# Weight rounding in place in four steps, and activation in ten lagged steps with two groups in flight

## The chip, the cores and the metric

The kernel runs on one core of a Trainium2 chip. Its time is the device time in microseconds of one execution; three runs of the kernel before gave 877.65, 879.63 and 879.96 us. The engines are TensorE (PE; its weight loads are PEld), VectorE (DVE), ScalarE (ACT), GpSimd (POOL) and SyncE (SP, which issues most DMAs).

## The reference

Two stages follow one another. The first is a gated recurrence for 4 batches, 8 heads, 768 steps and a head size of 48; its output, with heads side by side, is a matrix of 3072 rows and 384 columns. The second is a two-layer network with a softplus-erf activation:

```
f = 1 / (1 + exp(-f_logit))
state = f[t] * state + outer(k[t], v[t]);   y[t] = q[t] @ state
h = x @ w_in                      # 3072x384 @ 384x2048
g = h * erf(softplus(h))
out = g @ w_out                   # 3072x2048 @ 2048x384
```

The inputs q, k, v and f_logit are float32; the two weight matrices are float64.

## The kernel before, in words

**Blocks, chunks, groups.** The 3072 rows are cut into 8 blocks of 384, a block into 3 chunks of 128. For a chunk the recurrence is written as matrix products in four stages: `stage_d` (cumulated log gates through a triangular matmul, their exponentials `dp` and `dm`, and the scaled `qd` and `kd`), `stage_t` (transposes of `qd` and `kd` into `qT` and `kT`), `stage_s` (scores `sc`, masked into `A`, and the state's update `dS`, `Sn`, `Mbd`) and `stage_y` (the chunk's output, copied by ScalarE to `xT`). `prepare` and `prepare_log` take exp and log of a whole block's gates. In the network a block has 16 tiles of 128 hidden columns, in 4 groups of 4. `hidden` makes a group: 12 matmuls, and after each six a VectorE copy of two tiles from PSUM (`hps`, two buffers) into one of 7 buffers `Hg`. `activate` runs on a group of 128 x 1536 values: exp and log on ScalarE, four squares on ScalarE (L150), each followed by a product on VectorE (L155), tanh, and a last product. `project` multiplies a block's groups with `w_out`: 16 matmuls for each of three row tiles, a ScalarE copy `osb` and a DMA out.

**Slots.** The order of every instruction on every engine is written out by hand (a manual schedule); no planner moves anything. A loop over blocks `it` draws from `slots(it)`, a generator that issues one matmul of the network at a time: 48 slots in block 0 (its four groups), 96 in later blocks (three groups of block `it`, the projection of block `it - 1`, the fourth group), 48 in a last pass that only projects. Between slots the loop issues stages of the next block's chunks at even distances (some 7 slots in a full block), activation steps (`act_step`), loads, and in block 0 the rounding of the weights. Each engine runs what it was given in that order and waits where data is missing. When `project` needs a group that isn't activated yet, it issues activation steps until it is.

**Activation before.** `act_step` runs on every odd slot and advances the oldest group to its next `yield`; the next group starts when it has ended. A group takes 16 slots, so the four groups of a block take 64 of 96. A square and the product of the square before it are issued in one step. The squares have two buffers, tag `x`.

**Rounding before.** Each float64 weight arrives as two 32-bit words in a raw piece of 128 x 768 values (16 pieces, 8 of `w_in`, 8 of `w_out`), loaded into `Hg` buffers that activation doesn't use yet; `raw_buf` says which. `round_piece` makes float32 of it: `Abs` on ScalarE and a clamp on GpSimd into a scratch tile that takes the same two `x` buffers as the squares, then on VectorE four instructions with masks, shifts and a product (L239 to L249), and an add into the weight tile, on VectorE for `w_in`, on GpSimd for `w_out` (L254). `weights_step` ends the piece before and begins the next; when a piece has ended, its buffer is loaded with a later one.

Of the kernel before, what the change touches and what calls it, by code (L numbers as in the profile page):

```python
# [65 lines left out]
P = 128  # L66
# [3 lines left out]
def kernel(  # L70
# [18 lines left out]
    DP = 64  # L89
# [73 lines left out]
    work = main.enter_context(tc.tile_pool(name="work", bufs=2))  # L163
    work1 = main.enter_context(tc.tile_pool(name="work1", bufs=1))
# [40 lines left out]
    raw_buf = [0, 1, 2, 3, 4, 5, 6, 4, 5, 6, 4, 5, 6, 4, 5, 6]  # L205
# [17 lines left out]
    def round_piece(i):  # L223

        dst, raw = raws.pop(i)
        if wpe == 1:
            return
        words = raw.rearrange("p (n two) -> p n two", two=2)  # L230
        low, high = words[:, :, 0], words[:, :, 1]
        t = work.tile([P, 2, PIECE], U32, name="w_t", tag="x")
        x, z = t[:, 0, :], t[:, 1, :]
        nc.scalar.activation(out=x.bitcast(FP32), in_=high.bitcast(FP32), func=AF.Abs)  # L234
        nc.gpsimd.tensor_scalar(  # L235
            out=x.bitcast(FP32), in0=x.bitcast(FP32), scalar1=TINY, scalar2=None, op0=ALU.max
        )
        yield
        nc.vector.tensor_scalar(  # L239
            out=x, in0=x, scalar1=0x07FFFFFF, scalar2=3,  # L240
# [3 lines left out]
            out=x, in0=high, scalar=0xC0000000, in1=x, op0=ALU.bitwise_and, op1=ALU.bitwise_or  # L244
# [31 lines left out]
    def stage_d(g):  # L276
# [5 lines left out]
        dp = dps[g % 2]  # L282
# [11 lines left out]
            out=qds[g % 2][:, :, 0:D].rearrange("t (a r) d -> t a r d", r=2),  # L294
# [103 lines left out]

    def act_step():
# [8 lines left out]
    def hidden(blk, gi):  # L408

        gr = {"h": Hgs[n_made[0] % NG], "done": False}  # L410
        assert all(j < ended[0] for j, x in enumerate(raw_buf) if x == n_made[0] % NG)
        n_made[0] += 1
        groups[blk, gi] = gr
        for u in range(FG // 2):
            hps = ps_moe.tile([P, 2, 512], FP32, name="hps", tag="moe")
            for j in range(2):
                ft = gi * FG + 2 * u + j
                for kt in range(n_k):
# [6 lines left out]
                    if j == 1 and kt == n_k - 1:  # L425
                        nc.vector.tensor_copy(  # L426
# [68 lines left out]
    with tc.manual_schedule():  # L495
# [26 lines left out]
        for t in dps:  # L522
# [325 lines left out]
```

## Time and profile before

| | |
|---|---|
| median of 3 runs | 879.63 us (877.65 to 879.96) |
| the profiled execution | 878.28 us |
| its span, first to last instruction | 876.6 us |
| mean granted TensorE clock | 0.903 |
| busy: TensorE, ScalarE, VectorE, GpSimd | 684.9, 533.3, 504.7, 146.5 us |

A profile shows one execution. Busy times are unions of instructions, so engines overlap and their shares don't add to one. "Idle before" is the time for which an engine stood just ahead of an instruction, and the arrow names what released it. The clock is a share of TensorE's full speed. L12 is line 12 of the kernel.

### The profile page before, as it was taken

The page shows a single profiled execution, that of the slowest core. Times are in us where ns is not written, and L with a number is a line of the kernel's source. Part 1 is how long each engine was busy: PE and PEld are TensorE (multiplying, and loading weights), DVE is VectorE, ACT ScalarE, POOL GpSimd, SP SyncE. Part 2 cuts the span into 40 slices and gives each one's busy share as a digit, 9 for nine tenths or more (in the row PEclk, how much of TensorE's full clock was granted, in tenths as well). Part 3 has the DMA queues.
Part 4 walks back from the last instruction along what each step waited for, and adds up shares of the span by engine and source line. Part 5 has one row for each costly group of instructions (what it writes and reads, how often), then busy time and mean ns, then how long its engine had stood idle before and what let it go on. Part 6 is the DMA issues. An engine that isn't in the chain of part 4 may idle for free.

```text
span 876.6 us, 9159 instructions
## 1 busy us (share of the span) xinstructions
PE 684.9 (78%) x3729; PEld 410.2 (47%) x3729; DVE 504.7 (58%) x429; ACT 533.3 (61%) x457; POOL 146.5 (17%) x95
## 2 busy tenths in 40 slices
PE   3756636376888987978698886978698879989696
PEld 2524423244555554644455553644455545545353
DVE  3968775577562884277552884266552875185440
ACT  5264634277975779178745779178744776389450
POOL 2433445501210130000310130000310010000000
PEclk9868868779899899999899998999899999989999
DMA  9913145200113001400033001400030000000000
GB/s 222 261 49 93 45 105 147 35 1 0 37 37 63 1 1 37 99 0 1 1 73 63 1 1 37 99 0 1 1 73 10 1 0 19 10 1 0 18 10 30
DMA packets 112176, 36.88 MB, mean 42 GB/s; under 512 B 103936, under 2 KB 107008, under 8 KB 112128
## 3 DMA queue, kind: packets, MB, share of 16 engines
q1 hardware_dynamic: 108672, 36.18, 17.2%
q8 instruction: 31, 0.51, 0.2%
q10 hardware_dynamic: 3456, 0.05, 0.2%
q14 instruction: 17, 0.14, 0.1%
HBM read 31.46 MB, written 4.72 MB: 41 GB/s over the span
## 4 chain that ended last, share of the span: by engine, by line
ACT 29%; DVE 26%; PE 26%; issue 12%; POOL 4%; DMA 1%; ACTq 0%; SPq 0%; DVEq 0%; POOLq 0%
DVE e L155 17%; PE ops L445 15%; PE hps L419 7%; ACT x L150 5%; ACT yl L381 4%; ACT e L379 4%; ACT L381 3%; ACT e L394 3%; POOL w_out_sb L254 2%; ACT dp L285 2%; ACT L285 1%; PE y L144 1%; DVE Hg L426 1%; POOL w_t L235 1%; DVE qd L293 1%
## 5 line engine op out<-in xcount | busy, mean ns | idle before, releaser
L419 PE MATMUL hps<-xT,w_in_sb 128*128 128x384 f32 x768 | 290.9, 531 | 71.5 <-DVE Hg L426 65.1
L155 DVE SCALAR_TENSOR_TENSOR e<-x,e 128x1536 f32<-128x1536 f32 x128 | 244.2, 1908 | 109.7 <-ACT x L150 103.6
L445 PE MATMUL ops<-w_out_sb,Hg 128*128 128x384 f32 x768 | 274.0, 512 | 0.6 <-ACT osb L453 0.6
L419 PEld LDWEIGHTS hps<-xT,w_in_sb 128*128 128x128 f32 x768 | 154.4, 207 | 189.4 <-DVE Hg L426 71.8
L150 ACT ACTIVATE x<-yl,serf_bias 128x1536 f32<-128x1536 f32 x128 | 199.4, 1573 | 62.6 <-DVE e L155 44.3
L445 PEld LDWEIGHTS ops<-w_out_sb,Hg 128*128 128x128 f32 x768 | 151.6, 201 | 106.1 <-issue 19.5
L426 DVE COPY Hg<-hps 128x768 f32<-128x768 f32 x64 | 60.8, 951 | 94.5 <-PE hps L419 94.3
L298 POOL TENSOR_TENSOR kd<-kn,dm 128x384 f32<-128x384 f32 x24 | 32.6, 1360 | 421.6 <-ACT dm L289 257.2
L379 ACT ACTIVATE e<-Hg 128x1536 f32<-128x1536 f32 x32 | 47.2, 1475 | 63.9 <-DVE Hg L426 62.7
L394 ACT ACTIVATE e<-e 128x1536 f32<-128x1536 f32 x32 | 47.4, 1483 | 54.8 <-DVE e L155 53.8
L396 DVE TENSOR_TENSOR Hg<-Hg,e 128x1536 f32<-128x1536 f32 x32 | 62.3, 1946 | 22.0 <-ACT e L394 21.9
L293 DVE TENSOR_TENSOR qd<-qn,dp 128x384 f32<-128x384 f32 x24 | 20.6, 859 | 87.9 <-ACT dp L285 87.4
L279 PE MATMUL ps_d<-lt,tri 128*128 128x384 f32 x48 | 25.4, 617 | 40.0 <-ACT lt L274 40.0
L311 PE MATMUL ps_t<-ident,kd 128*128 128x128 f32 x96 | 19.4, 339 | 42.0 <-DVE Sn L356 38.9
L144 PE MATMUL y<-A,vt 128*32 128x128 f32 x768 | 39.0, 295 | 16.4 <-DVE kT L316 15.1
L381 ACT ACTIVATE yl<-e 128x1536 f32<-128x1536 f32 x32 | 47.5, 1483 | 0.4
L359 POOL TENSOR_TENSOR Mbd<-Sn,Tall 48x192 f32<-48x192 f32 x32 | 30.3, 947 | 99.7 <-DVE Sn L356 98.5
L144 PEld LDWEIGHTS y<-A,vt 128*32 128x32 f32 x768 | 29.4, 115 | 29.7 <-DVE kT L316 17.1
L235 POOL TENSOR_SCALAR w_t<-w_t 128x768 f32<-128x768 f32 x16 | 37.3, 2332 | 26.8 <-ACT w_t L234 26.7
L381 ACT ACT_TABLE_LOAD x32 | 41.1, 1283 | 0.6
L370 ACT COPY xT<-y 128x384 f32<-128x384 f32 x24 | 11.3, 471 | 43.8 <-PE y L144 43.8
L234 ACT ACTIVATE w_t<-Hg 128x768 f32<-128x768 f32 x16 | 14.3, 903 | 35.9 <-POOL w_out_sb L254 28.6
(53 smaller groups left out, 496.2 us busy)
## 6 DMA issues: line engine op xcount, KB each, us to landing
Hg<-in_moe_w_in_dram SPq DMA_DIRECT2D x8, 768.0 KB, 6.7
Hg<-in_moe_w_out_dram SPq DMA_DIRECT2D x8, 768.0 KB, 4.4
lt<-in_f_logit_dram SPq DMA_DIRECT2D x24, 192.0 KB, 3.6
qn<-in_q_dram SPq DMA_DIRECT2D x24, 192.0 KB, 3.6
kn<-in_k_dram SPq DMA_DIRECT2D x24, 192.0 KB, 3.8
vt<-in_v_dram SPq DMA_DIRECT2D x24, 192.0 KB, 3.8
out_dram<-osb SPq DMA_DIRECT2D x24, 192.0 KB, 2.0
Tall<-dp ACTq DMA_DIRECT2D x24, 2.0 KB, 2.0
```

The source lines that it names most:

```text
L144: nc.tensor.matmul(y[M * i : M * (i + 1), kt, :], lhsT=terms[n][0], rhs=terms[n][1], start=(n == 0), stop=(n == len(terms) - 1), skip_grou ...
L150: nc.scalar.activation(out=dst[:], in_=y[:], func=AF.Square, bias=serf_bias[:, i : i + 1], scale=SERF_K)
L155: nc.vector.scalar_tensor_tensor(out=e[:], in0=x[:], scalar=SERF_AB[i][1], in1=e[:], op0=ALU.add, op1=ALU.mult)
L235: nc.gpsimd.tensor_scalar(out=x.bitcast(FP32), in0=x.bitcast(FP32), scalar1=TINY, scalar2=None, op0=ALU.max)
L298: nc.gpsimd.tensor_tensor(out=kds[g % 2][:, :, 0:D], in0=kns[g % NQ][:].rearrange("t (h d) -> t h d", d=D), in1=dm[:].rearrange("t (h d) - ...
L379: nc.scalar.activation(out=e[:], in_=h, func=AF.Exp)
L381: nc.scalar.activation(out=y[:], in_=e[:], func=AF.Ln, scale=SERF_C, bias=1.0)
L394: nc.scalar.activation(out=e[:], in_=e[:], func=AF.Tanh)
L396: nc.vector.tensor_tensor(out=h, in0=h, in1=e[:], op=ALU.mult)
L419: nc.tensor.matmul(hps[:, j, 0:TB], lhsT=w_in_sb[:, kt, ft * P : (ft + 1) * P], rhs=xTs[blk][:, kt, :], start=(kt == 0), stop=(kt == n_k - 1),
L426: nc.vector.tensor_copy(out=gr["h"][:, 2 * u : 2 * u + 2, :], in_=hps[:, :, 0:TB])
L445: nc.tensor.matmul(of[tt], lhsT=gr["h"][:, ft % FG, tt * P : (tt + 1) * P], rhs=w_out_sb[:, ft, :], start=(ft == 0), stop=(ft == n_ft - 1),)
```

## The change

- **Rounding** uses no scratch: `Abs` writes into the weight tile itself, the clamp and the masks work there, and the masked exponent goes back into the raw words (`high`, every second word). Its parts lie in separate steps: `Abs`; clamp; the four VectorE instructions; the add. The add is VectorE's for the first three pieces and GpSimd's for the other 13. `weights_step` advances every piece in flight by one step. Buffers for the pieces are given out in another order.
- **Activation** has ten steps: exp; log; four squares with the products two steps behind them, over six steps; tanh; the last product. A second group starts when the first has done six steps, and both are advanced in one `act_step`. Squares have three buffers of their own (`xpool`). Steps come on every third slot in blocks 0 and 1, on every fourth afterwards, and on every slot in the last pass.
- `qd` and `dp` have one buffer instead of two.
- Loads of the gates of block 1 are issued ahead of the fourth weight piece, q, k, v of chunks 3 and 4 within the first chunks' stages, and exp and log of block 1's gates before `stage_y(2)`; the stages of block 0 start at slot 3 instead of 12.

```diff
+    xpool = main.enter_context(tc.tile_pool(name="xpool", bufs=3))
...
-    qds = [fixed(f"qd{i}", [P, H, DP], pool=fix) for i in range(2)]
+    qd = fixed("qd", [P, H, DP], pool=fix)
-    dps = [fixed(f"dp{i}", [P, 2, DP, HP], pool=fix) for i in range(2)]
+    dp = fixed("dp", [P, 2, DP, HP], pool=fix)
...
-    raw_buf = [0, 1, 2, 3, 4, 5, 6, 4, 5, 6, 4, 5, 6, 4, 5, 6]
+    FIRST_PIECES = 3
+    raw_buf = [0, 1, 2, 3, 4, 5, 6, 3, 4, 5, 6, 4, 5, 6, 4, 5]
...
     def round_piece(i):
-        words = raw.rearrange("p (n two) -> p n two", two=2)
-        low, high = words[:, :, 0], words[:, :, 1]
-        t = work.tile([P, 2, PIECE], U32, name="w_t", tag="x")
-        x, z = t[:, 0, :], t[:, 1, :]
-        nc.scalar.activation(out=x.bitcast(FP32), in_=high.bitcast(FP32), func=AF.Abs)
-        nc.gpsimd.tensor_scalar(
-            out=x.bitcast(FP32), in0=x.bitcast(FP32), scalar1=TINY, scalar2=None, op0=ALU.max
-        )
+        m = dst.shape[1]
+        words = raw.rearrange("p (a n two) -> p a n two", a=m, two=2)
+        low, high = words[:, :, :, 0], words[:, :, :, 1]
+        bits = dst.bitcast(U32)
+        nc.scalar.activation(out=dst, in_=high.bitcast(FP32), func=AF.Abs)
+        yield
+        nc.gpsimd.tensor_scalar(out=dst, in0=dst, scalar1=TINY, scalar2=None, op0=ALU.max)
         yield
...
         nc.vector.tensor_scalar(
-            out=z, in0=x, scalar1=0xFF800000, scalar2=None, op0=ALU.bitwise_and
+            out=high, in0=bits, scalar1=0xFF800000, scalar2=None, op0=ALU.bitwise_and
         )
...
-        eng = nc.vector if i < n_pieces else nc.gpsimd
-        eng.tensor_tensor(
-            out=dst,
...
+        if i >= FIRST_PIECES:
+            yield
+        (nc.vector if i < FIRST_PIECES else nc.gpsimd).tensor_tensor(
+            out=dst, in0=low.bitcast(FP32), in1=dst, op=ALU.add
         )
...
     def activate(gr):
         nc.scalar.activation(out=e[:], in_=h, func=AF.Exp)
+        yield
         y = work1.tile([P, FG * TB], FP32, name="yl", tag="yl")
         nc.scalar.activation(out=y[:], in_=e[:], func=AF.Ln, scale=SERF_C, bias=1.0)
         yield
-        x = None
-        for i in range(len(SERF_AB)):
-            x_new = work.tile([P, FG * TB], FP32, name="x", tag="x")
-            squared(x_new, y, i)
-            if x is not None:
-                times(e, x, i - 1)
-            x = x_new
+        n = len(SERF_AB)
+        xs = {}
+        for i in range(n + 2):
+            if i < n:
+                xs[i] = xpool.tile([P, FG * TB], FP32, name="x", tag="x")
+                squared(xs[i], y, i)
+            if i >= 2:
+                times(e, xs.pop(i - 2), i - 2)
             yield
-        times(e, x, len(SERF_AB) - 1)
-        yield
-        yield
         nc.scalar.activation(out=e[:], in_=e[:], func=AF.Tanh)
         yield
         nc.vector.tensor_tensor(out=h, in0=h, in1=e[:], op=ALU.mult)
...
+    LEAD = len(SERF_AB) + 2
+    running = []
     def act_step():
-        while acts:
-            if next(acts[0], "end") != "end":
-                return
-            acts.popleft()
+        if acts and (not running or running[-1][1] >= LEAD):
+            running.append([acts.popleft(), 0])
+        for r in list(running):
+            r[1] += 1
+            if next(r[0], "end") == "end":
+                running.remove(r)
...
-        next_piece(5)
+        for g in range(CPB, 2 * CPB):
+            load_f(g)
+        next_piece(2)
...
-        def weights_step():
-            if rounding:
-                next(rounding.popleft(), None)
-                ended[0] += 1
-                next_piece()
-            if begun[0] < 2 * n_pieces:
+        def weights_step(begin=True):
+            for r in list(rounding):
+                if next(r, "end") == "end":
+                    rounding.remove(r)
+                    ended[0] += 1
+            if begin and begun[0] in raws:
                 rounding.append(round_piece(begun[0]))
                 next(rounding[-1], None)
                 begun[0] += 1
+            next_piece()
...
+        load_to(LOOK)
+        next_piece()
         stage_s(0)
...
         stage_s(1)
+        weights_step()
         stage_t(2)
+        stage_y(1)
         weights_step()
-        stage_y(1)
         stage_s(2)
-        load_to(LOOK)
+        prepare(1, 0, CPB)
         weights_step()
+        prepare_log(1, 0, CPB)
         stage_y(2)
...
-            first = 12 if it == 0 else 2
+            first = 3
...
-                if it == 0 and s % (6 if s < 25 else 3) == 1 or (it, s) == (1, 1):
+                if it == 0 and s % (6 if s < 24 else 3) == 1 or it == 1 and s < 12:
                     weights_step()
...
-                if s % 2:
+                if s % (3 if it < 2 else 4) == 2 or it == n_blocks:
                     act_step()
...
-            while it == n_blocks and acts:
-                act_step()
```

## Rows read from the trace of the kernel before

**Rows 1.** The page, part 1: busy us, share of the span, instructions.

```profile
PE 684.9 (78%) x3729; PEld 410.2 (47%) x3729; DVE 504.7 (58%) x429; ACT 533.3 (61%) x457; POOL 146.5 (17%) x95
```

**Rows 2.** Busy time by stretch: length, engines, TensorE clock, DMA share, GB/s.

```profile
core 0: us, PE busy (x) PEld busy (x) DVE busy (x) ACT busy (x) POOL busy (x), PEclk, DMA share, GB/s
0.00:39.50 39.50, 20.09 (x271) 14.38 (x271) 23.40 (x45) 16.24 (x21) 15.17 (x20) 0.91 0.99 247
39.50:139.60 100.10, 60.66 (x384) 37.36 (x384) 74.41 (x75) 49.48 (x49) 43.40 (x22) 0.78 0.33 84
139.60:204.90 65.30, 36.49 (x150) 20.65 (x150) 42.12 (x39) 37.04 (x30) 20.48 (x9) 0.76 0.18 43
204.90:271.00 66.10, 54.26 (x315) 32.82 (x314) 37.97 (x27) 45.34 (x40) 10.68 (x7) 0.90 0.22 45
271.00:368.60 97.60, 84.34 (x471) 50.44 (x470) 55.40 (x41) 64.63 (x55) 13.32 (x8) 0.93 0.14 30
...
566.30:666.10 99.80, 83.78 (x463) 50.17 (x462) 56.09 (x43) 64.64 (x55) 12.02 (x8) 0.93 0.09 19
666.10:758.00 91.90, 80.32 (x462) 48.66 (x461) 51.32 (x39) 58.38 (x48) 6.04 (x6) 0.94 0.02 7
758.00:838.10 80.10, 68.09 (x193) 38.41 (x192) 43.65 (x30) 59.70 (x43) 0.00 (x0) 0.94 0.02 5
838.10:876.60 38.50, 31.53 (x98) 18.05 (x96) 8.78 (x8) 8.56 (x9) 0.00 (x0) 0.97 0.06 23
```

**Rows 3.** Waits of TensorE: total us, times, longest.

```profile
PE hps L419 <- DVE Hg L426: 65.1, 23, 10.9
...
PE ps_d L279 <- ACT lt L274: 40.0, 7, 10.7
PE ps_t L311 <- DVE Sn L356: 38.9, 9, 7.0
```

**Rows 4.** Timeline of TensorE at three places: start us, length us.

```profile
52.40 1.65 PE L279 MATMUL ps_d<-lt,tri 128*128 128x384 f32 x2 [3.42 <-ACT lt L274]
...
460.61 9.84 PE L419 MATMUL hps<-xT,w_in_sb 128*128 128x384 f32 x30
...
830.39 33.70 PE L445 MATMUL ops<-w_out_sb,Hg 128*128 128x384 f32 x104
```

**Rows 5.** Lines of 39.5 to 204.9 us: busy us, mean ns, idle before.

```profile
L155 DVE SCALAR_TENSOR_TENSOR e<-x,e 128x1536 f32<-128x1536 f32 x16 | 31.1, 1944 | 7.6 <-ACT x L150 7.4
...
L150 ACT ACTIVATE x<-yl,serf_bias 128x1536 f32<-128x1536 f32 x16 | 25.1, 1574 | 27.3 <-POOL w_out_sb L254 11.8 <-DVE e L155 11.3 <-DVE w_in_sb L254 3.9
L254 POOL TENSOR_TENSOR w_out_sb<-Hg,w_t 128x768 f32<-128x768 f32 x8 | 20.5, 2566 | 28.3 <-DVE Hg L249 23.5 <-issue 4.8
...
L234 ACT ACTIVATE w_t<-Hg 128x768 f32<-128x768 f32 x12 | 10.7, 902 | 34.8 <-POOL w_out_sb L254 28.6 <-DVE w_in_sb L254 5.9 <-ACT dm L289 0.2
L239 DVE TENSOR_SCALAR w_t<-w_t 128x768 uint32<-128x768 uint32 x13 | 10.0, 766 | 15.9 <-POOL w_t L235 15.9
...
L396 DVE TENSOR_TENSOR Hg<-Hg,e 128x1536 f32<-128x1536 f32 x4 | 7.3, 1826 | 1.1 <-ACT e L394 1.1
...
L254 DVE TENSOR_TENSOR w_in_sb<-Hg,w_t 128x768 f32<-128x768 f32 x6 | 5.7, 958 | 0.2
...
L293 DVE TENSOR_TENSOR qd<-qn,dp 128x384 f32<-128x384 f32 x5 | 4.2, 848 | 19.8 <-ACT dp L285 19.8
...
L270 ACT ACTIVATE lt<-lt 128x1152 f32<-128x1152 f32 x2 | 2.3, 1164 | 10.1 <-DVE lt L267 5.3 <-POOL lt L267 4.9
```

**Rows 6.** Single lines: ns shortest/median/longest; last: all table loads of L381.

```profile
L155 DVE SCALAR_TENSOR_TENSOR e<-x,e x128: 1741/1758/4250, 70.6 to 843.1; 128x1536 f32<-128x1536 f32 x128
...
L246 DVE TENSOR_SCALAR w_t<-w_t x16: 559/560/1060, 23.9 to 168.8; 128x768 uint32<-128x768 uint32 x16
...
L249 DVE SCALAR_TENSOR_TENSOR Hg<-Hg,w_t x16: 958/959/960, 24.5 to 169.4; 128x768 f32<-128x768 uint32 x16
...
L381 ACT ACT_TABLE_LOAD x32 | 41.1, 1283 | 0.6
```

More of the change, by code (lines that the diff above doesn't have):

```diff
@@ L243, in round_piece @@
         nc.vector.scalar_tensor_tensor(
-            out=x, in0=high, scalar=0xC0000000, in1=x, op0=ALU.bitwise_and, op1=ALU.bitwise_or
+            out=bits, in0=high, scalar=0xC0000000, in1=bits, op0=ALU.bitwise_and, op1=ALU.bitwise_or
         )
         nc.vector.tensor_scalar(
-            out=z, in0=x, scalar1=0xFF800000, scalar2=None, op0=ALU.bitwise_and
+            out=high, in0=bits, scalar1=0xFF800000, scalar2=None, op0=ALU.bitwise_and
         )
         nc.vector.scalar_tensor_tensor(
-            out=low.bitcast(FP32), in0=low, scalar=2.0**-52, in1=z.bitcast(FP32),
+            out=low.bitcast(FP32), in0=low, scalar=2.0**-52, in1=high.bitcast(FP32),
             op0=ALU.mult, op1=ALU.mult,
         )
-        eng = nc.vector if i < n_pieces else nc.gpsimd
-        eng.tensor_tensor(
-            out=dst,
-            in0=low.bitcast(FP32).rearrange("p (a f) -> p a f", a=dst.shape[1]),
-            in1=x.bitcast(FP32).rearrange("p (a f) -> p a f", a=dst.shape[1]),
-            op=ALU.add,
+        if i >= FIRST_PIECES:
+            yield
+        (nc.vector if i < FIRST_PIECES else nc.gpsimd).tensor_tensor(
+            out=dst, in0=low.bitcast(FP32), in1=dst, op=ALU.add
         )
@@ L306, in stage_t @@
         pss = []
-        for src in (qds[g % 2], kds[g % 2]):
+        for src in (qd, kds[g % 2]):
             ps = ps_at.tile([P, HP, P], FP32, name="ps_t", tag="at")
@@ L410, in hidden @@
         gr = {"h": Hgs[n_made[0] % NG], "done": False}
-        assert all(j < ended[0] for j, x in enumerate(raw_buf) if x == n_made[0] % NG)
+        own = n_made[0] % NG
         n_made[0] += 1
@@ L425, in hidden @@
                     if j == 1 and kt == n_k - 1:
+                        assert all(i < ended[0] for i, x in enumerate(raw_buf) if x == own)
                         nc.vector.tensor_copy(
@@ L508 @@
             load_f(g)
-        load(0)
-        next_piece()
-        load(1)
-        next_piece()
-        load(2)
-        next_piece(5)
+        for g in range(LOOK):
+            load(g)
+            next_piece()
+        for g in range(CPB, 2 * CPB):
+            load_f(g)
+        next_piece(2)
         nc.gpsimd.memset(tri[:], 1.0)
@@ L521 @@
         make_identity(nc, ident)
-        for t in dps:
-            nc.vector.memset(t[:, :, D:DP, :], 1.0)
-        for t in qds + kds:
+        nc.vector.memset(dp[:, :, D:DP, :], 1.0)
+        for t in [qd] + kds:
             nc.vector.memset(t[:, :, D:DP], 0.0)
@@ L529 @@
             nc.vector.memset(t[:], 0.0)
-        rounding = deque()
+        rounding = []
         begun = [0]
-        def weights_step():
-            if rounding:
-                next(rounding.popleft(), None)
-                ended[0] += 1
-                next_piece()
-            if begun[0] < 2 * n_pieces:
+        def weights_step(begin=True):
[4 more added lines that the diff above has]
+            if begin and begun[0] in raws:
                 rounding.append(round_piece(begun[0]))
@@ L560 @@
         stage_d(1)
+        load_to(LOOK)
+        next_piece()
         stage_s(0)
@@ L595 @@
             n = n_slots[it]
-            first = 12 if it == 0 else 2
+            first = 3
             at = [int(first + (n - 10 - first) / max(1, len(todo)) * i) for i in range(len(todo))]
             for s, _ in enumerate(slots(it)):
-                if it == 0 and s % (6 if s < 25 else 3) == 1 or (it, s) == (1, 1):
+                if it == 0 and s % (6 if s < 24 else 3) == 1 or it == 1 and s < 12:
                     weights_step()
-                if it == 0 and s in (0, 6):
-                    load_to(4 + s // 6)
-                    if s == 6:
-                        prepare(1, 0, CPB)
-                        prepare_log(1, 0, CPB)
+                if (it, s) == (0, 2):
+                    load_to(LOOK + 2)
                 if at and s == at[0]:
```

9 lines of the change are left out of this document (4 added, 5 removed).

## The prediction

> **What bounds the kernel now.** I read the page's first part first [rows 1]: TensorE is the busiest engine but idle for a fifth of the span, and no other engine passes 61%. An average over unlike stages says little, so I cut the span at the block boundaries, found in the timeline of TensorE by counting the matmuls on `hps` and `ops` (each appears as two rows), and asked for the busy time and clock of each cut [rows 2]. The reader is to see four kinds of stretch:
> - a prologue of 39.5 us with the DMA share at 0.99;
> - block 0 (100.1 us) and the first three hidden groups of block 1 (65.3 us). TensorE is busy 60.7 and 36.5 us at clocks of 0.78 and 0.76, VectorE 74.4 and 42.1. This is where the weights are rounded, and VectorE, the busiest engine, still idles for 165.4 - 116.5 = 48.9 us;
> - the rest of block 1 (66.1 us), then four steady blocks of 97.6 to 99.8 us (first and last shown; together 666.1 - 271.0 = 395.1 us) and the shorter blocks 6 and 7 (91.9 and 80.1);
> - 38.5 us for the last projection and the flag.
>
> In a steady block TensorE is busy 84.3 us at 0.93. At full clock that work is 84.34 x 0.93 = 78.4 us; the other end gives 83.78 x 0.93 = 77.9. I take 78. ScalarE has 64.6 us of work there and VectorE 55.4 to 56.1, so both would fit beside TensorE. The block is 20 us longer than 78 because activation is bunched: 64 of 96 slots carry it, then none. The waits say the same [rows 3]: TensorE stands 65.1 us for the PSUM copy that queues behind products on VectorE, 40.0 us for ScalarE's log of the forget gates, 38.9 us for VectorE's `Sn`. After a stand the clock is low too: the two matmul rows after the 3.4 us stand at 52.4 us take 1.65 us, while 30 take 9.84 us and 104 take 33.70 us in unbroken runs (0.33 us each) [rows 4]. That last run also shows TensorE at full clock for 34 us on end.
>
> **The change part by part.**
>
> *Steady blocks.* A group now takes ten steps and the next starts with its seventh, so a group costs six steps; four groups make 24, and a step falls on every fourth of 96 slots. The activation work is unchanged but lies evenly over the block. Each product trails its square by two steps instead of one, with three `x` buffers. One step is a 78 / 24 = 3.25 us share of the block; ScalarE's share is 64.6 / 24 = 2.7 us and VectorE's 56 / 24 = 2.3. The heaviest step (table load 1.28, tanh and square 1.6 each) is 4.5 us, 1.2 us over its share, and the two steps after it are one square each, so the backlog drains. In the hidden phase VectorE gets between two PSUM copies (six slots, 3.9 us) one copy and one or two products of 1.76 us [rows 6], at most 4.5 us, with two PSUM buffers to lend another 3.9. So I expect nearly all of the 65.1 us stand to go. Next late is ScalarE at mid-block: the gate's exp and log, two table loads, tanh and three chunk copies fall within 16 slots, some 17 us against 13. That is 4 to 5 us of lag where the projection's own PSUM leaves 4 to 8 of slack. I allow 1.5 us a block: 79.5 each, 318 for four (floor 4 x 77.7 = 311; with half of the gain 4 x 88.5 = 354). Block 6 is 80.32 x 0.94 = 75.5, plus 1: 76.5. Block 7 is 68.09 x 0.94 = 64, plus 3 where its last hidden group has one PSUM buffer: 67 (62 to 74).
>
> Does ScalarE still fit? The trace shows 32 loads before the log, 1.283 us each, with 0.6 us of idle time in all before them [rows 6]. The order of the new steps still switches twice a group and twice for the gates, about ten loads a block, as before. The Trainium skill ("ScalarE: Activation LUTs", What ACT_TABLE_LOAD costs) speaks against the change here: it puts a switch at about 2.66 us, as a drain of 1.38 us goes with the load. By it ScalarE's 64.6 us would be about 78.4, as much as TensorE, and each of its waits would be added; I would call that an estimate of 84 us a block and 755 us in all. The rows show no such drain, and the measurement decides.
>
> *Rounding: block 0 and the first part of block 1.* Here VectorE is the work to count. In the stretch [rows 5] it does 20 products (16 + 4) and six adds of pieces on `w_in_sb` (5.7 us). By the new order I count 18 products and no such add there: five adds move to GpSimd, which has slack (43.4 of 100.1 us busy), at 2.57 us each. The masked exponent is written back into the raw words with stride 2. The trace has no such instruction: the contiguous one takes 0.56 us, and an instruction that writes these words with two inputs 0.96 [rows 6]. So it costs 0 to 0.4 us each, 13 times here, 0 to 5.2 us; a gain is excluded, since the contiguous form is the fastest row of that size. I take 0, as it stays a one-input instruction. VectorE: 116.5 - 5.7 - 2 x 1.9 = 107 us (to 112).
>
> What the stretch loses beside that is waiting [rows 5]: ScalarE stands 34.8 us before `Abs` (28.6 for GpSimd's add) and 27.3 before squares (11.8 for the same add), because the rounding's scratch shares the two `x` buffers with the squares. VectorE in turn stands 15.9 us for GpSimd's clamp and 19.8 for `dp`. In place, the scratch is gone; `Abs` waits for its DMA alone, and the clamp now has a whole step before VectorE needs it. If those two waits of VectorE go, 35.7 of the 48.9 us of idle time go with them, and 107 + 13 = 120 is left; I take 122. Ends: 107 if VectorE never waits, 153 if it idles for 30% as now. The new cover is thin: a reloaded piece's `Abs` stands in ScalarE's fixed order, and if the DMA lands late, the squares queued behind it wait, then the products, then the PSUM copies, then TensorE.
>
> GpSimd beside VectorE is the second price. A product's median is 1.758 us and its longest 4.250 [rows 6], in the stretch its mean is 1.944 [rows 5]. The Trainium skill ("SBUF — State Buffer", SBUF: two separate sides) says why this can grow: GpSimd and a two-input VectorE instruction share a port that the first takes for its whole length. By it five more adds could block VectorE for up to 5 x 2.57 = 12.8 us, and the stretch would be 135, which lies inside the ends above; the mean shows 0.2 us a product, so I keep 122.
>
> *Rest of block 1.* Steps run every third slot here. ScalarE has 22 passes over whole groups instead of 17: 45.3 + 5 x 1.57 = 53 us, above TensorE's 54.26 x 0.90 = 49. I take 54 (49 to 62) against 66.1.
>
> *Prologue.* The gates' exp and log of block 1 move ahead of the third `xT` copy: two passes of 1.16, one load of 1.28 and an `Abs` of 0.9, some 4.5 us on ScalarE before the first hidden matmul. The third piece's five VectorE instructions now lie there too, beside TensorE. The gates' DMAs go three places earlier on SP's queue, which holds the third and fourth piece back by 0.6 MB, 2 to 3 us, before they are read. I take +4: 43.5 (39.5 to 46). What it buys lies in block 0: the stand for the log at 52.4 us goes.
>
> *End.* All ten steps of the last group, and the last four of the one before, now run inside the last projection, one per slot. Tanh of the older group comes behind the younger one's exp and log: three passes of 1.57, two loads and a product are 9.0 us, and the ninth matmul needs it after 8 x 0.65 = 5.2. So 3.8 us of waiting and about 1 of low clock: 38.5 + 5 = 43.5 (38.5 to 46). The last group has 36 matmuls (23 us) over it and is ready in time.
>
> *At nothing.* One `qd` and one `dp` instead of two: the next write is a whole chunk later, 28 slots in a steady block and some 5 us in the prologue, with readers that take 0.9 us and a DMA of 2 us; uncovered it would be 1 to 2 us a chunk in block 0 only. Piece loads wait on SP for GpSimd's add as before; behind them stand q, k, v of a chunk three ahead.
>
> **Sum.** 43.5 + 122 + 54 + 318 + 76.5 + 67 + 43.5 = 724.5 us of span, and 1.7 around it (878.28 - 876.6) is 726. The median of the runs lies 1.35 above the profiled one: 728.
>
> **Rivals.**
> - *Spreading moves the stand instead of removing it.* Engines run in fixed order, and one late product still holds the PSUM copy: half of the gain comes, blocks take 88.5. For it: ScalarE would be 83% full and its mid-block burst stays. Against: no wait in [rows 3] is for an engine that is full. 728 + 4 x 9 + 4 + 5 + 4 = 777.
> - *The rounding chain stays as it is.* Abs, clamp, four instructions, add, reload over three buffers end the stretch, not `x`: it keeps its 165.4, and the total is 728 + 43 = 771. For it: GpSimd's load grows by 13 us. Against: those buffers come round every 12 slots, over 20 us at VectorE's pace, and the chain itself is near 15.
> - *Slower: the two groups put ScalarE and VectorE in step.* Old and young group alternate on both queues, so each step could wait for the other engine. Without overlap a steady block would be 64.6 + 55.4 = 120 us, four of them 480 against 318, and some 65 more in blocks 6 and 7: 728 + 227 = 955. It makes the kernel slower from 26 us more in each of the six blocks, about 105. Against: today these engines overlap even with a lag of one step.
> - *The change doesn't do what it says*: the lag of two finds its square still missing. Then only the even spread is left, which is the first rival.
>
> **How the numbers follow.** The forecast (all parts, 690 to 760) has 0.73, the first rival 0.14, the rounding rival 0.07, the slower one 0.03; 0.03 is left for faster than 690. If all terms fall at one end together they add to 685 and 822; 8 in 10 is 690 to 785. Faster by over 0.3% (2.6 us, what a measurement of this kernel can tell): 0.96; within: 0.01; slower: 0.03.
>
> **What would show it.** Right: blocks 2 to 5 near 80 us with TensorE's clock at 0.97 or more, the stand for the PSUM copy under 20 us in all, still 32 loads before the log, `Abs` hardly waiting for GpSimd, and the stretch of rounding near 120. Wrong: a clock below 0.9 in unbroken runs, table loads well over ten a block, or TensorE standing for the PSUM copy in every hidden phase.

## The result and the profile after

The changed kernel takes 728.62 us (727.14 to 729.77, four runs) against 879.8 us: a ratio of 0.8276 with a 95% interval of 0.8242 to 0.8311. The forecast was 728. Two of its terms were wrong by 10 us each, with opposite signs, and the half of the change that isn't activation turned out to be worth nothing beside it.

The page's busy line of the kernel after; it answers to [rows 1]:

```profile
PE 644.3 (89%) x3729; PEld 394.8 (54%) x3729; DVE 507.3 (70%) x422; ACT 525.2 (72%) x455; POOL 163.3 (23%) x100
```

TensorE rose from 78% to 89%, though its busy time fell by 40.6 us: the same matmuls ran at a higher clock. The cuts of the kernel after, by length, busy time of PE, PEld, DVE, ACT and POOL, clock, DMA share and GB/s; they answer to [rows 2] one for one, with blocks 2 and 5 for the four steady ones:

```profile
0.00:45.90 45.90, 20.65 (x271) 14.92 (x271) 27.78 (x46) 20.66 (x26) 19.23 (x21) 0.89 0.93 229
45.90:119.90 74.00, 56.05 (x384) 34.65 (x384) 65.86 (x59) 42.60 (x43) 49.56 (x24) 0.89 0.40 98
119.90:177.60 57.70, 37.05 (x148) 21.06 (x149) 51.59 (x43) 32.75 (x28) 25.77 (x11) 0.79 0.21 56
177.60:232.00 54.40, 50.39 (x315) 30.98 (x314) 40.84 (x30) 49.25 (x43) 10.68 (x7) 0.97 0.21 46
232.00:309.90 77.90, 77.32 (x472) 47.83 (x471) 52.04 (x41) 61.43 (x53) 11.91 (x8) 1.00 0.22 45
...
463.70:540.50 76.80, 76.80 (x463) 47.65 (x462) 54.52 (x44) 64.05 (x56) 13.42 (x8) 1.00 0.14 30
540.50:616.00 75.50, 75.42 (x460) 46.40 (x459) 50.29 (x40) 57.58 (x49) 7.45 (x6) 1.00 0.03 9
616.00:679.60 63.60, 62.55 (x195) 36.59 (x194) 44.62 (x31) 53.00 (x39) 0.00 (x0) 1.00 0.02 7
679.60:725.40 45.80, 34.26 (x98) 19.20 (x96) 13.27 (x11) 16.18 (x14) 0.00 (x0) 0.88 0.05 19
```

Prologue and end grew by 6.4 and 7.3 us; every other stretch fell. The steady blocks (308.5 us for four, 395.1 before) have TensorE busy for all but 0.6 us at a clock of 1.00: there is next to nothing left in them but matmuls. ScalarE and VectorE do about the work they did before, beside it. The waits that answer to [rows 3], and one that is new (total us, times, longest):

```profile
PE hps L425 <- DVE Hg L433: 26.0, 6, 9.4
...
ACT w_out_sb L237 <- DMA Hg<-in_moe_w_out_dram: 20.8, 6, 7.1
...
PE ps_d L279 <- ACT lt L274: 10.9, 1, 10.9
...
PE ps_t L310 <- DVE Sn L355: 6.8, 3, 5.3
```

The stand for the PSUM copy fell from 65.1 to 26.0 us, of which 24.4 lie in the stretch of rounding; the stands for the log and for `Sn` fell from 40.0 and 38.9 to 10.9 and 6.8.

### The profile page after: what moved, and what is told of

Read it like the earlier page. It is cut to its first block, busy times and chain, and to the rows that moved or that the text cites. A ratio compares the mean times of both kernels' runs of the same rounds, so it can differ in the third digit from the quotient of the medians.

```text
span 725.4 us, 9143 instructions
## 1 busy us (share of the span) xinstructions
PE 644.3 (89%) x3729; PEld 394.8 (54%) x3729; DVE 507.3 (70%) x422; ACT 525.2 (72%) x455; POOL 163.3 (23%) x100
## 4 chain that ended last, share of the span: by engine, by line
PE 64%; DVE 14%; ACT 11%; issue 5%; POOL 3%; DMA 2%; SPq 0%; ACTq 0%; DVEq 0%; POOLq 0%
PE ops L452 30%; PE hps L425 24%; DVE e L155 4%; PE y L144 3%; ACT x L150 2%; PE sc L323 2%; PE ps_t L310 2%; PE ps_d L279 1%; DVE Hg L248 1%; ACT e L379 1%; DVE w_out_sb L241 1%; ACT yl L382 1%; DVE w_out_sb L245 1%; DVE qd L292 1%; ACT e L393 1%
## 5 line engine op out<-in xcount | busy, mean ns | idle before, releaser
L425 PE MATMUL hps<-xT,w_in_sb 128*128 128x384 f32 x768 | 271.7, 507 | 29.4 <-DVE Hg L433 26.0
L452 PE MATMUL ops<-w_out_sb,Hg 128*128 128x384 f32 x768 | 263.2, 496 | 8.7 <-DVE Hg L395 8.2
L155 DVE SCALAR_TENSOR_TENSOR e<-x,e 128x1536 f32<-128x1536 f32 x128 | 240.1, 1876 | 6.3 <-ACT x L150 1.1
L425 PEld LDWEIGHTS hps<-xT,w_in_sb 128*128 128x128 f32 x768 | 148.1, 197 | 133.3 <-DVE Hg L433 24.2
L452 PEld LDWEIGHTS ops<-w_out_sb,Hg 128*128 128x128 f32 x768 | 144.8, 193 | 107.7 <-DVE Hg L395 9.4
L144 PEld LDWEIGHTS y<-A,vt 128*32 128x32 f32 x768 | 29.7, 115 | 19.2 <-issue 11.8
L328 DVE TENSOR_TENSOR A<-sc,mask 128x1024 f32<-128x1024 f32 x24 | 29.3, 1219 | 10.2 <-PE sc L323 10.0
L284 ACT ACTIVATE dp<-ps_d 128x384 f32<-128x384 f32 x24 | 20.6, 859 | 18.0 <-PE ps_d L279 16.4
L144 PE MATMUL y<-qT,Mbd 128*32 128x128 f32 x480 | 33.1, 290 | 0.0
L323 PEld LDWEIGHTS sc<-qT,kT 48*128 48x128 f32 x384 | 23.7, 190 | 16.2 <-issue 12.5
L279 PE MATMUL ps_d<-lt,tri 128*128 128x384 f32 x48 | 21.4, 530 | 10.9 <-ACT lt L274 10.9
```

Source lines behind the costliest of these rows:

```text
L144: nc.tensor.matmul(y[M * i : M * (i + 1), kt, :], lhsT=terms[n][0], rhs=terms[n][1], start=(n == 0), stop=(n == len(terms) - 1), skip_grou ...
L155: nc.vector.scalar_tensor_tensor(out=e[:], in0=x[:], scalar=SERF_AB[i][1], in1=e[:], op0=ALU.add, op1=ALU.mult)
L323: nc.tensor.matmul(sc[:, r, a, :], lhsT=kT[rows(r), a, :], rhs=qT[rows(r), a, :], start=True, stop=True,)
L425: nc.tensor.matmul(hps[:, j, 0:TB], lhsT=w_in_sb[:, kt, ft * P : (ft + 1) * P], rhs=xTs[blk][:, kt, :], start=(kt == 0), stop=(kt == n_k - 1),
L452: nc.tensor.matmul(of[tt], lhsT=gr["h"][:, ft % FG, tt * P : (tt + 1) * P], rhs=w_out_sb[:, ft, :], start=(ft == 0), stop=(ft == n_ft - 1),)
```

## The experiments

All were timed on a chip beside the kernel before. The table cuts each profile as above: first matmul on `hps`, first on `ops`, then block by block (a block ends 24 matmul rows, 7.74 us at full clock, after TensorE turns from `ops` to `hps`; block 7 ends as long after the last turn from `hps` to `ops`). "Both" is prologue and rounding together. Each cut is of one profile: seven kernels with the same program up to the first hidden matmul (changed, only_round, one_group, lag_one, no_reload, add_vec, tail) have prologues of 45.8 to 48.5 us, so 2 or 3 us in a cut prove nothing by themselves. "Theory" and "rival" are the two outcomes named before a run.

| kernel | median us | ratio (95%) | prologue | rounding | both | rest of 1 | mean of 2-5 | 6 | 7 | end |
|---|---|---|---|---|---|---|---|---|---|---|
| before | 879.8 | | 39.5 | 165.4 | 204.9 | 66.1 | 98.8 | 91.9 | 80.1 | 38.5 |
| changed | 728.62 | 0.8276 (0.8242-0.8311) | 45.9 | 131.7 | 177.6 | 54.4 | 77.1 | 75.5 | 63.6 | 45.8 |
| only_act | 728.58 | 0.8276 (0.8253-0.8300) | 39.5 | 140.0 | 179.5 | 54.6 | 76.9 | 75.5 | 63.6 | 45.9 |
| only_round | 863.32 | 0.9810 (0.9781-0.9838) | 46.3 | 145.1 | 191.4 | 66.7 | 98.8 | 89.3 | 81.4 | 38.4 |
| split_x | 865.53 | 0.9849 (0.9822-0.9876) | 39.5 | 152.4 | 191.9 | 66.1 | 98.7 | 91.9 | 80.1 | 38.4 |
| one_group | 777.83 | 0.8844 (0.8812-0.8876) | 45.8 | 144.5 | 190.3 | 71.0 | 83.6 | 77.7 | 64.2 | 38.5 |
| lag_one | 731.75 | 0.8318 (0.8297-0.8338) | 48.5 | 132.1 | 180.6 | 59.6 | 77.7 | 75.5 | 63.2 | 40.0 |
| no_reload | 727.97 | 0.8270 (0.8238-0.8301) | 46.5 | 131.9 | 178.4 | 54.4 | 77.1 | 75.5 | 63.6 | 45.4 |
| add_vec | 724.24 | 0.8213 (0.8185-0.8240) | 48.3 | 127.1 | 175.4 | 54.5 | 77.2 | 75.4 | 63.6 | 45.3 |
| no_clamp | 723.06 | 0.8197 (0.8158-0.8236) | 47.8 | 125.0 | 172.9 | 54.4 | 77.1 | 75.5 | 63.6 | 45.4 |
| tail | 723.38 | 0.8214 (0.8186-0.8243) | 46.2 | 132.2 | 178.5 | 56.2 | 77.1 | 75.4 | 63.6 | 39.0 |
| prologue | 729.59 | 0.8290 (0.8269-0.8310) | 39.6 | 140.0 | 179.6 | 54.4 | 77.1 | 75.5 | 63.6 | 46.2 |
| best | 718.50 | 0.8162 (0.8145-0.8179) | 42.3 | 133.8 | 176.1 | 54.8 | 77.2 | 75.5 | 63.6 | 38.6 |
| best_vec | 720.88 | 0.8179 (0.8156-0.8202) | 45.6 | 134.6 | 180.2 | 55.0 | 77.2 | 75.5 | 63.6 | 38.1 |

### Either half alone

**only_act**: the kernel before with the new `activate`, `act_step`, pool and step distances.

```diff
+    xpool = main.enter_context(tc.tile_pool(name="xpool", bufs=3))
...
-                if s % 2:
+                if s % (3 if it < 2 else 4) == 2 or it == n_blocks:
```

> The kernel before with the ten lagged steps, two groups in flight, three buffers for squares and the new step distances alone; rounding, loads and prologue as before. Theory (the two parts add up, each acting in its own stretch): the steady blocks take 77 us as with the whole change (308 for four instead of 395), blocks 6 and 7 about 76 and 64, the end 46, the rest of block 1 about 55, and the prologue and the stretch of rounding stay near 39.5 and 165: about 755 us, 745 to 765. Rival (the squares' own buffers, not the rounding in place, undo the wait in the rounding stretch): the stretch falls to 140 or less and the total to 730 or less.

**only_round**: the changed kernel with the old `activate`, `act_step` and odd slots.

```diff
-    xpool = main.enter_context(tc.tile_pool(name="xpool", bufs=3))
...
-                if s % (3 if it < 2 else 4) == 2 or it == n_blocks:
+                if s % 2:
```

> The changed kernel with the old activation: one group at a time on every odd slot, products one step behind, two buffers for squares. Theory (parts add up): steady blocks return to 97 to 100 us, and what is left is the stretch of rounding (132 instead of 165) less 6 in the prologue: about 852 us, 840 to 865. Rival (rounding gains only because activation no longer fills VectorE there): the stretch stays at 150 or more and the total at 870 or more.

The parts don't add up as the theory had it. only_act has the whole gain, 728.58 us, with the rounding and all else untouched; these are the rival's numbers, and split_x tests the rival's reason. Its windows, prologue, rounding and a steady block:

```profile
0.00:39.50 39.50, 20.10 (x271) 14.37 (x271) 23.38 (x45) 16.24 (x21) 15.16 (x20) 0.91 0.95 242
39.50:179.50 140.00, 92.88 (x533) 54.99 (x534) 113.64 (x110) 79.39 (x74) 68.22 (x31) 0.82 0.32 82
...
234.10:311.10 77.00, 77.00 (x471) 47.87 (x470) 52.86 (x41) 61.32 (x53) 11.95 (x8) 1.00 0.22 45
```

The stretch fell to 140.0 and did not stay at 165. only_round, with 863.3 in all, is within the theory's 840 to 865, but its stretch came to 145.1 and not to 132: a gain of 20.3 us. So the gains there are 25.4 and 20.3 apart and 33.7 together, as if both undid the same thing in part. And the 8.3 us that rounding in place adds to only_act's stretch (140.0 to 131.7) are spent in its prologue (39.5 to 45.9): 1.9 us stay in the profile and nothing in the medians.

### What both halves undo

**split_x**: the kernel before, with two buffers for the squares that the rounding's scratch doesn't use.

```diff
+    xpool = main.enter_context(tc.tile_pool(name="xpool", bufs=2))
-            x_new = work.tile([P, FG * TB], FP32, name="x", tag="x")
+            x_new = xpool.tile([P, FG * TB], FP32, name="x", tag="x")
```

> The kernel before with two buffers of their own for the squares; the rounding's scratch keeps the two it had, nothing else is changed. Theory (the shared buffers are what both halves of the change undo, which is why their gains in the stretch don't add up: 25.4 and 20.3 apart, 33.7 together): ScalarE no longer waits for GpSimd's add before squares and the stretch falls from 165 to 150 or less, the rest stays: 860 to 867 us. Rival (the pace of activation made the gain, not the buffers): the stretch stays above 160 and the total within 4 us of 880.

The stretch came to 152.4, 2.4 over what the theory allowed, and the total to 865.5, within it. Lines of that stretch (busy us, mean ns | idle before):

```profile
L150 ACT ACTIVATE x<-yl,serf_bias 128x1536 f32<-128x1536 f32 x16 | 25.1, 1574 | 17.2 <-DVE e L155 16.9 <-ACT dm L290 0.2
...
L235 ACT ACTIVATE w_t<-Hg 128x768 f32<-128x768 f32 x12 | 10.8, 903 | 23.6 <-POOL w_out_sb L255 19.8 <-DVE w_in_sb L255 3.1 <-POOL w_t L236 0.3
```

The squares' wait for GpSimd's add, 11.8 us in [rows 5], is gone; `Abs` still waits for it. Shared buffers explain 13 us of the stretch, about half of what only_act gains there. The other half comes from the rest of the new activation: 13 products on `e` fall into the stretch instead of 16, VectorE stands 0.3 us before them instead of 7.6, and the squares have a third buffer. It was not taken apart further.

### Lag and overlap

**lag_one**: products one step behind.

```diff
-        for i in range(n + 2):
+        for i in range(n + 1):
...
-            if i >= 2:
-                times(e, xs.pop(i - 2), i - 2)
+            if i >= 1:
+                times(e, xs.pop(i - 1), i - 1)
```

> The changed kernel with each product one step behind its square instead of two (nine steps a group, overlap and step distances kept). Theory (the lag of two covers ScalarE's backlog of 4 to 5 us at mid-block): VectorE waits for squares again, copies and scores come late, and a block takes 1 to 2 us more: 735 to 742. Rival (a step of 3.2 us is longer than a square, so one step is enough): within 3 us of 729.

731.75 us, 3.1 more, with an interval that overlaps the changed kernel's: within the rival's range. A steady block takes 77.7 instead of 77.1; the rest of block 1 loses 5, and the end, with one step less, gains 6. Leaving out the lag of two costs next to nothing.

**one_group**: one group at a time, spread as evenly.

```diff
-        if acts and (not running or running[-1][1] >= LEAD):
+        if acts and (not running or running[-1][1] >= 99):
...
-                if s % (3 if it < 2 else 4) == 2 or it == n_blocks:
+                if s % 12 in (1, 4, 6, 9, 11) or it < 2 and s % 2 or it == n_blocks:
```

> The changed kernel with activation spread as evenly but one group at a time: ten steps a group, 40 steps over the 96 slots (five in twelve), on every odd slot in blocks 0 and 1. Theory (overlap of two groups is needed): inside one group ScalarE stands some 3.5 us for the last two products before tanh, so its 64.6 us become about 79 a block, over TensorE's 77: blocks of 80 to 83 us, 745 to 765 in all. Rival (even spreading alone is what counts): blocks stay at 77 and the time within 5 us of the changed kernel's 729, apart from 2 to 4 us in blocks 0 and 1.

In blocks 0 and 1 the edit gives steps on two even slots of each twelve beside the odd ones. The kernel takes 777.8 us, 49 more and beyond the theory's 765: steady blocks take 79.6 and 87.5 in turn, the stretch of rounding loses 13 and the rest of block 1 loses 17. Waits in block 3 of it, one of the longer ones:

```profile
ACT e L393 <- DVE e L155: 17.6, 5, 6.5
...
PE ps_t L310 <- DVE Sn L355: 4.8, 1, 4.8
...
PE hps L425 <- DVE Hg L433: 2.8, 3, 1.3
```

ScalarE stands 17.6 us before tanh for the last products, as the theory had it for four groups (14 us), and the transposes stand 4.8 us for `Sn`, the stand that [rows 3] showed; that the one leads to the other, and why blocks alternate, isn't shown. Without overlap two thirds of the change's gain are left; overlap is worth the rest. The even distance and the third buffer for squares were not tested alone.

### What sets the stretch of rounding

In these three the first fence is the stretch's row (length, busy PE, PEld, DVE, ACT, POOL); lines of single instructions give busy us, mean ns and idle before.

**no_reload**:

```diff
-        nc.sync.dma_start(out=to, in_=src.rearrange("(t p) w -> p t w", p=P))
+        if i < 7:
+            nc.sync.dma_start(out=to, in_=src.rearrange("(t p) w -> p t w", p=P))
```

> The changed kernel without the DMAs of the nine pieces that are loaded into buffers a second time (those pieces round what lies there, so the weights are not the real ones); every other instruction stays. In the changed kernel ScalarE stands 20.8 us at Abs for these DMAs. Theory D (ScalarE's fixed order hands these waits on to products, copies and TensorE): the stretch of rounding falls from 132 to about 118, VectorE's busy time there: 715 us, 710 to 720. Theory P (VectorE's own time, lengthened by GpSimd, sets the stretch, and the DMA waits are idle time of an engine with slack): 128 or more, 725 or more.

```profile
46.50:178.40 131.90, 91.49 (x533) 54.87 (x534) 117.46 (x102) 74.77 (x71) 75.33 (x34) 0.84 0.13 24
```

It came out as theory P had it: 131.9 us, the same. The 20.8 us that ScalarE stands for DMAs cost nothing; without them it stands for VectorE's products instead (30.8 us before tanh and squares, 14.5 in the changed kernel).

**no_clamp**:

```diff
-        nc.gpsimd.tensor_scalar(out=dst, in0=dst, scalar1=TINY, scalar2=None, op0=ALU.max)
```

> The changed kernel without GpSimd's clamp of the 16 pieces (it changes only weights below 0.00003 in size); the steps stay. GpSimd has some 31 us less in the stretch. Theory P (GpSimd's port holds up VectorE): the first masking instruction falls from 1.4 to about 0.6 us, VectorE's busy time from 117 to about 107, and the stretch to 115 to 122: 712 to 719 us. Theory D (the reload DMAs set the stretch; the clamp has a step of its own to hide in): the stretch within 4 us of 132, total 725 to 733.

```profile
47.80:172.90 125.10, 90.53 (x533) 54.45 (x534) 113.56 (x102) 75.39 (x71) 44.16 (x23) 0.85 0.33 83
```

The stretch took 125.0 us, 6.7 less, and the total is 723.06: both between what the two theories named (122 and 128, 719 and 725), so neither is borne out. Prologue and stretch together fell by 4.7. VectorE's busy time fell by 3.9, not 10. Its first masking instruction, which was to fall to 0.6 us, still takes 1.10 on the `w_out` pieces (1.33 with the clamp) and 1.55 on those of `w_in`, as with the clamp:

```profile
L240 DVE TENSOR_SCALAR w_out_sb<-w_out_sb 128x768 uint32<-128x768 uint32 x8 | 8.8, 1095 | 0.0
L240 DVE TENSOR_SCALAR w_in_sb<-w_in_sb 128x768 uint32<-128x768 uint32 x5 | 7.8, 1554 | 0.0
```

**add_vec**:

```diff
-        (nc.vector if i < FIRST_PIECES else nc.gpsimd).tensor_tensor(
+        nc.vector.tensor_tensor(
```

> The changed kernel with the adds of the 13 later pieces on VectorE instead of GpSimd, in the same steps: 13 x 0.96 = 12.5 us more for VectorE, 32 us less for GpSimd. Theory P (each GpSimd instruction beside VectorE lengthens VectorE's by about as much as the add costs there): the stretch stays within 4 us of 132, and the total at 725 to 733. Rival (VectorE's count of work sets the stretch, and GpSimd is free help): 12 us more, 741.

```profile
48.30:175.40 127.10, 89.79 (x532) 53.51 (x533) 116.39 (x115) 74.88 (x70) 39.23 (x21) 0.86 0.32 81
```

127.1 us, and 724.24 in all: VectorE took over 13 adds and was busy 1.1 us less, as GpSimd was busy 36 us less. Here the first masking instruction falls to 0.76 and 0.98 us:

```profile
L241 DVE TENSOR_SCALAR w_out_sb<-w_out_sb 128x768 uint32<-128x768 uint32 x8 | 6.1, 760 | 0.0
L241 DVE TENSOR_SCALAR w_in_sb<-w_in_sb 128x768 uint32<-128x768 uint32 x5 | 4.9, 979 | 0.0
```

It was GpSimd's adds that lengthened it, and not its clamps, as theory P of no_clamp had it. Giving the 13 adds to GpSimd is a loss; the five that the change moves there were not tested alone.

### End, prologue, and a version that beats both

**tail**:

```diff
-        return project(last, list(range(CPB)), [range(n_ft - FG), range(n_ft - FG, n_ft)])
+        return project(last, list(range(CPB)), [range(2 * FG), range(2 * FG, 3 * FG), range(3 * FG, n_ft)])
```

> The changed kernel with the last projection in the order: the first two groups for all three row tiles, then the third group for all, then the fourth. The ninth matmul no longer needs the third group, the 25th does. Theory (the 4.2 us stand of TensorE after eight matmuls and the low clock behind it are the whole cost of the end): 45.8 becomes 39 to 41, total 723 to 725. Rival (the stand moves to the fourth group, whose chain starts no earlier): 727 to 730.

TensorE's rows at the end, first of the changed kernel, then of this one (start, length):

```profile
671.85 13.06 PE L452 MATMUL ops<-w_out_sb,Hg 128*128 128x384 f32 x40
689.09 23.41 PE L452 MATMUL ops<-w_out_sb,Hg 128*128 128x384 f32 x64 [4.17 <-DVE Hg L395]
```

```profile
674.18 33.70 PE L452 MATMUL ops<-w_out_sb,Hg 128*128 128x384 f32 x104
```

The stand of 4.17 us is gone, and 104 matmul rows run through at 0.32 us each; in the changed kernel the 64 rows behind the stand take 0.37, at a granted clock of 0.89 instead of 1.00. The end fell by 6.8 us to 39.0, the median by 5.2.

**prologue**:

```diff
         stage_s(1)
+        prepare(1, 0, CPB)
         weights_step()
         stage_t(2)
+        prepare_log(1, 0, CPB)
         stage_y(1)
-        weights_step()
         stage_s(2)
-        prepare(1, 0, CPB)
         weights_step()
-        prepare_log(1, 0, CPB)
+        weights_step()
         stage_y(2)
```

> The changed kernel with exp and log of block 1's gates taken earlier in the prologue, where ScalarE stands 7.9 us, and the second piece's VectorE instructions behind the scores of the third chunk. Theory (the gates and the pieces ahead of the last xT copy are the 6.4 us that the prologue grew by): first hidden matmul at 39 to 42 us instead of 46, and 3 to 6 us less in all: 723 to 726. Rival (the DMAs set the prologue, or the work only moves into block 0): prologue and stretch together stay at 177 to 179 us, total 727 to 730.

It came out as the rival had it. The prologue fell to 39.6 us and the stretch rose to 140.0, 179.6 together. Rows cut at 42 us show where the work went:

```profile
0.00:42.00 42.00, 21.68 (x278) 15.12 (x279) 22.64 (x41) 22.53 (x27) 15.59 (x20) 0.96 0.94 234
42.00:178.00 136.00, 88.40 (x522) 53.16 (x521) 121.44 (x107) 71.82 (x67) 78.74 (x36) 0.82 0.33 82
```

VectorE does 144.1 us of work by 178 us, wherever the cut lies (145.2 by 177.6 in the changed kernel, 27.78 + 117.45): the edit moved work over the border and removed none. That VectorE's sum alone sets when the first projection begins isn't shown: in only_act it is 137.0 us (23.38 + 113.64), and the projection begins no earlier, at 179.5.

**best**: tail, prologue, and all adds on VectorE in the masking step. **best_vec** takes the clamp from GpSimd too. Their edits beside those above, the first fence for both, the second for best_vec alone:

```diff
-        if i >= FIRST_PIECES:
-            yield
-        (nc.vector if i < FIRST_PIECES else nc.gpsimd).tensor_tensor(
+        nc.vector.tensor_tensor(
```

```diff
         yield
-        nc.gpsimd.tensor_scalar(out=dst, in0=dst, scalar1=TINY, scalar2=None, op0=ALU.max)
         yield
+        nc.vector.tensor_scalar(out=dst, in0=dst, scalar1=TINY, scalar2=None, op0=ALU.max)
```

> Three edits together: the other order of the last projection, the other order in the prologue, and all adds of pieces on VectorE in the same step as the four masking instructions. If they add up: 728.6 - 5.2 (end) - 4.4 (adds) - 3 to 6 (prologue) = 713 to 716 us. If the prologue gives nothing: 719.

> The same three edits with the clamp on VectorE too, so that GpSimd takes no part in rounding: VectorE gets 13 clamps of 0.56 to 0.95 us in the stretch, some 9 us more, GpSimd loses 31. Theory P (GpSimd's instructions cost VectorE about as much as they save): within 3 us of the run with the clamp on GpSimd. Rival (with the adds gone, GpSimd has stopped being in the way): 6 to 9 us slower than that run.

best takes 718.5 us, 0.8162 (0.8145 to 0.8179) of the kernel before and clear of the changed kernel's interval. The prologue's part gives nothing, and for that case the text had 719; the adds in one step less gave no more than in add_vec (176.1 for both stretches, 175.4 there). best_vec is 2.4 us slower, within theory P's 3, and the intervals overlap. With all 16 clamps, 11 us of work, VectorE is busy for 148.2 us up to the first projection, against 145.4 in best: GpSimd's clamps save it about 3 us.

## Why the prediction was right, and where it was not

Its terms against the profile, in the order of its sum: prologue 43.5 and 45.9, rounding 122 and 131.7, rest of block 1 54 and 54.4, four steady blocks 318 and 308.5, block 6 76.5 and 75.5, block 7 67 and 63.6, end 43.5 and 45.8. The errors are +2.4, +9.7, +0.4, -9.5, -1.0, -3.4 and +2.3: the total is met within 1 us because they cancel, and that is luck.

**Steady blocks: right, and better.** The reading of [rows 2], that 78 us of matmuls lay in a block of 98 because activation was bunched, held within 1 us: 77.1 on average, below the floor of 77.7. The 1.5 us allowed for stands were not needed: from block 2 to block 6 TensorE stands 0.6 us in all, and the clock stays at 1.00. What ScalarE is late by at mid-block therefore reaches TensorE nowhere. The dearer table switch of the Trainium skill ("ScalarE: Activation LUTs", What ACT_TABLE_LOAD costs) would, by the prediction's estimate of 78.4 us, have made ScalarE the bound; this case goes by the row, in which 31 loads have 1.8 us of idle time before all of them:

```profile
L382 ACT ACT_TABLE_LOAD x31 | 39.8, 1283 | 1.8 <-ACT dm L288 1.3
```

**Lag: a reason that failed.** The text let the lag of two steps carry the gain beside the spreading. lag_one shows that it is worth 0.6 us a block, and one_group that the overlap, which the text counted as a way to get 24 steps, is worth 6.5 us a block and more in block 1.

**Rounding: the mis-sized step.** "VectorE: 116.5 - 5.7 - 2 x 1.9 = 107 us" measured 117.5, while its idle time came out as said: 14.2 against 13. Lines of the stretch in the kernel after (busy us, mean ns | idle before), beside [rows 5]:

```profile
L155 DVE SCALAR_TENSOR_TENSOR e<-x,e 128x1536 f32<-128x1536 f32 x13 | 27.2, 2093 | 0.3
L239 POOL TENSOR_SCALAR w_out_sb<-w_out_sb 128x768 f32<-128x768 f32 x8 | 23.7, 2974 | 0.0
...
L257 POOL TENSOR_TENSOR w_out_sb<-Hg,w_out_sb 128x768 f32<-128x768 f32 x8 | 19.9, 2487 | 17.2 <-DVE Hg L251 17.2
L257 POOL TENSOR_TENSOR w_in_sb<-Hg,w_in_sb 128x768 f32<-128x768 f32 x5 | 12.1, 2430 | 1.7 <-DVE Hg L251 1.6
L241 DVE TENSOR_SCALAR w_out_sb<-w_out_sb 128x768 uint32<-128x768 uint32 x8 | 10.6, 1330 | 4.0 <-POOL w_out_sb L239 4.0
L241 DVE TENSOR_SCALAR w_in_sb<-w_in_sb 128x768 uint32<-128x768 uint32 x5 | 7.8, 1552 | 0.0
...
L292 DVE TENSOR_TENSOR qd<-qn,dp 128x384 f32<-128x384 f32 x5 | 6.7, 1348 | 4.6 <-ACT dp L284 4.6
L395 DVE TENSOR_TENSOR Hg<-Hg,e 128x1536 f32<-128x1536 f32 x3 | 6.3, 2087 | 1.7 <-ACT e L393 1.7
```

There are 16 products (13 and 3) and not 18, each dearer than before on average (2.09 us instead of 1.94 and 1.83), and together 33.5 us, no more than the 34.6 that the sum left for 18. The surplus lies elsewhere: the first masking instruction takes 1.33 to 1.55 us where it took 0.77, some 8 us more over 13 pieces, and the product for `qd` 1.35 where it took 0.85, 2.5 us more. GpSimd was busy for 75.3 of these 131.7 us (63.9 of 165.4 before). One masking instruction with nothing beside it, then GpSimd's add and one that begins while it runs (start, length):

```profile
46.13 0.68 DVE L241 TENSOR_SCALAR w_in_sb<-w_in_sb 128x768 uint32<-128x768 uint32 x1
...
85.39 3.12 POOL L257 TENSOR_TENSOR w_in_sb<-Hg,w_in_sb 128x768 f32<-128x768 f32 x1
86.72 2.34 DVE L241 TENSOR_SCALAR w_in_sb<-w_in_sb 128x768 uint32<-128x768 uint32 x1
```

The second ends 0.55 us after the add. Seven of the 13 begin while a GpSimd instruction with two inputs runs (six times an add), and each ends 0.42 to 0.55 us after that one; the other six take 0.54 to 1.17 us. The change puts the add one step behind its piece, into the step in which the next piece is masked, so the two often meet.

The prediction had the price in the sentence on the port and left it out of the sum, because one row, the products' mean, showed only 0.2 us. That row came from a stretch with less of GpSimd in it, and other instructions paid. The prediction's estimate of 135 us by the Trainium skill ("SBUF — State Buffer", SBUF: two separate sides: the shared port is held for a whole instruction) was nearer than the 122 taken. The trace agrees for adds, by the seven instructions above, and add_vec, where 4.6 us of the stretch come back and VectorE does 13 adds more in less time. Beside clamps it doesn't: one masking instruction begins and ends within a clamp and takes 0.54 us. Another 1 us is the shape of one write (last section).

**Rounding: the wrong owner.** That the scratch's shared buffers held up the squares was right (split_x: 13 us). That it takes rounding in place to free them was not: `xpool`, which activation brings, frees them as well. The prediction never asked what each half would give alone.

**The cover it called thin was not.** `Abs` does stand 20.8 us for reloads, as feared; no_reload shows that the stretch doesn't get shorter without it. The rival of the rounding chain falls with the stretch, which did not keep its 165.4 us.

**Prologue.** +4 was said and +6.4 came. Read alone, the term misleads: the run prologue shows that what leaves it returns in the stretch behind. Counted with the stretch, the term was 165.5 against 177.6.

**Rest of block 1: met, but not for the reason given.** 54 was said and 54.4 came, but not by ScalarE's 53 us of work: it did 49.3. TensorE has 50.4 us there and stands 4.0 for an activation's last product.

**End.** The chain of 9.0 us against 5.2 gave 3.8; the stand was 4.17. Its price was 7, not 5, as tail shows: the 64 rows behind the stand, at a clock of 0.89, take 2.7 us more than at 1.00.

**The other rivals.** Spreading did not move the stand, and the engines did not fall into step: in the steady blocks TensorE waits 0.6 us in all.

## What to carry to other kernels

Find the stretch in which the bounding engine is idle though no engine is full, and spread and overlap the work of the others over the whole period; here that, with buffers of their own for the squares, gave the whole gain. Count an engine's work to the point that all must reach, over stage borders: a term that shrinks may only have handed its work to its neighbour. Before giving work to GpSimd, weigh what it adds to VectorE's instructions beside it, in the stretch where it will run, and look which of them begin while it runs.

## What the runs showed of the hardware

The write of the masked exponent with stride 2 costs nothing by its stride, but by its shape. Single instructions of that line in the kernel after (ns shortest/median/longest):

```profile
L248 DVE TENSOR_SCALAR Hg<-w_in_sb x8: 953/954/985, 29.5 to 90.3; 128x768 uint32<-128x768 uint32 x8
L248 DVE TENSOR_SCALAR Hg<-w_out_sb x8: 560/561/869, 97.6 to 150.3; 128x768 uint32<-128x768 uint32 x8
```

For pieces of `w_out` (two rows of 384 values in the source, end to end) it takes 0.56 us, as the contiguous form did in [rows 6]; for pieces of `w_in` (three rows of 256, apart) 0.954. The target runs through all 768 values at one stride in both. The Trainium skill ("VectorE: DVE Perf Modes", Mode 2×_2P) asks for an outermost dimension that is even, or odd and equal in source and target, for the two-port rate; three rows against one run is neither, and the trace agrees: the first masking instruction, which has three rows in both, takes 0.68 us where nothing runs beside it (46.13 above). The shape adds 0.4 us to eight pieces, 3 us in all.

TensorE held its upper clock (1.00, 2.4 GHz, in every cut from block 2 to block 7) for 448 us, busy for all but 2 of them.
